# The first twenty weight loads of a fused attention and feed-forward kernel, each issued as two transfers of 64 partitions

## The chip, the cores and the metric

The kernel runs on one core of a Trainium2 chip. The metric is the device time of one execution in microseconds, and lower is better. Three runs of the kernel before gave 1049.2, 1049.21 and 1049.95 us, with a median of 1049.21.

The core's engines go through their own instruction streams in order and meet at semaphores: TensorE (PE) multiplies, and loads its stationary operand beside that (PEld); VectorE (DVE) and ScalarE (ACT) work element by element; SyncE (SP) issues nearly all the DMA transfers. Sixteen DMA engines move the data between HBM and the 128 partitions of the on-chip memory.

## The reference

The first part is a linear attention over 8 batches, 8 heads and 576 positions of 64 numbers, with 256 features for each position:

```python
def phi(x):
    proj = np.einsum('bhsd,df->bhsf', x, w_phi)
    proj = proj - np.max(np.abs(proj), axis=-1, keepdims=True)
    return np.concatenate([np.exp(proj), np.exp(-proj)], axis=-1)
q_p, k_p = (phi(q), phi(k))
kv = np.einsum('bhsf,bhsd->bhfd', k_p, v)
z = np.sum(k_p, axis=2)
num = np.einsum('bhsf,bhfd->bhsd', q_p, kv)
den = np.einsum('bhsf,bhf->bhs', q_p, z)[..., None] + 1e-06
attn_out = (num / den).astype(np.float32)
```

Its output, as 4608 tokens of 512 numbers, goes through a feed-forward layer whose two weight matrices (512 x 2048 and 2048 x 512) arrive in float64:

```python
h = x @ w_in
sp = np.where(h > 20.0, h, np.log1p(np.exp(np.minimum(h, 20.0))))
g = h * np.tanh(sp)
out = (g @ w_out).astype(np.float32)
```

## The kernel before

**The two stages.** Keys and queries are loaded in units of 512 positions (`load_raw`, tiles `raw_k` and `raw_q`, 256 KB). TensorE projects a unit (`pp_k`, `pp_q`), VectorE finds the largest magnitude (`m_k`, `m_q`) and subtracts it (`e_k`, `e_q`), and ScalarE takes the exponentials. Key features times values (`v`, 330 KB a batch and pair of heads) are summed on TensorE in `kvps` and copied to `kv`. Query features are turned (`dt`), multiplied with `kv` (`num`), and divided on VectorE (`r`, `x`). The result is turned to `xt` and split into a high part `xTh` (ScalarE) and a low part `xTl` (VectorE). The feed-forward stage works on 18 chunks of 256 tokens, each with 16 column tiles: `h` is x times w_in, `u` its activation, `o` the product with w_out. Each factor is held in a high and a low part, so that one product takes three. From the fourth chunk on, `o` is formed from sums and differences of blocks (`ox`, `oy`, `oz`, `ow`), for which sums of the weights are made on the chip, kept in HBM (`terms`) and loaded again.

**The weights.** They come as 32 pieces, 16 of w_in (`words_in`) and 16 of w_out (`words_out`), of 128 rows of 512 float64 numbers: 4 KB a partition, 512 KB a piece. `load_weight` (L242) brings the words of a piece. For 29 of the pieces `load_middle` (L246) brings a second copy, shifted by 16 bits, into one of three homes (`middle_in`, `middle_out`, 4092 bytes a partition), so that VectorE can take the lower bits of the mantissa from it. For each piece ScalarE takes the magnitude of the high words (L251, waits for the words). VectorE then clamps (L265), shifts the middle copy (L270, waits for it), shifts (L278), sets the sign (L283, waits for the words), cuts out the power of two (L288) and writes the low part of the weight (L293). ScalarE writes the high part (L312). A home is free for the next shifted copy when L293 of the piece before is done, and SP waits for that.

**What sets the order.** A planner (class `Plan`) simulates the engines with a table of due times and durations and then writes out the order of every engine's instructions, loads included. It plans one task for each load of words or of a shifted copy. `load_weight` and `load_middle` are called in the planned order, and what a task issues does not change the plan. SP goes through its list in order: an instruction that has to wait holds up all those behind it.

**The semaphores of the transfers.** The transfers of SP and ScalarE take eight semaphores in turn (DMAHW0 to DMAHW7). A transfer that would take a semaphore again first waits until the transfer that had it before has landed. So at most eight are under way, and the ninth is issued when the first has landed. Each transfer is spread over the sixteen DMA engines.

**The first 60 us.** SP issues keys, queries and values first, and the first words (`words_in`) at 5.91 us. Until 22 us it issues the words of the first nine pieces and the shifted copies of the first three among queries and values. The shifted copies of further pieces wait for a home from 29.84 us on. TensorE works on attention until the first `h` at 46.8 us.

Of the kernel before, what the change touches and what calls it, by code (L numbers as in the profile page):

```python
# [10 lines left out]
U32 = mybir.dt.uint32  # L11
U16 = mybir.dt.uint16
# [5 lines left out]
P = 128  # L18
# [41 lines left out]
NFIRST = 6  # L60
NTRIAL = 3
NLOADS = 11
VLATE = 4.5
E0 = 0.138
E1 = 0.171
# [20 lines left out]
class Plan:  # L86
# [11 lines left out]
    def order(self):  # L98
# [85 lines left out]
        tasks = [task for _, _, task in issued]  # L184
        at = [n for n, task in enumerate(tasks) if task["name"].startswith("load ")][:NLOADS]
        loads = sorted(range(NLOADS), key=lambda i: i + VLATE * tasks[at[i]]["name"].startswith("load v"))
        for n, task in zip(at, [tasks[at[i]] for i in loads]):
# [5 lines left out]
def attention_then_mish(ctx, tc, qT, kT, va, w_phi, w_in, w_out, out):  # L193
    nc = tc.nc
# [28 lines left out]
    def slot_tile(slot, dtype, name, words=None):  # L223
        return const.tile([P, words] if words else [P, 2, 512], dtype, tag=slot, name=name)
# [11 lines left out]
    def octets(kind, i, j):  # L236
        return w_in[i * P:(i + 1) * P, j * 512:(j + 1) * 512] if kind == "in" else w_out[i * P:(i + 1) * P, :]

    def load_weight(kind, i, j):
        nm = f"{kind}_{i}_{j}"  # L240
        words = weight[kind, i, j] = slot_tile(f"w{nm}", U32, f"words_{nm}").rearrange("p a b -> p (a b)")
        nc.sync.dma_start(words, octets(kind, i, j).bitcast(U32))  # L242

    def load_middle(kind, i, j, home):
        middle = middles[kind, i, j] = slot_tile(home, U16, f"middle_{kind}_{i}_{j}", 2048)
        nc.sync.dma_start(middle[:, :2046], octets(kind, i, j).bitcast(U16)[:, 1:2047])  # L246

    def magnitude(kind, i, j):
        w = to_add[kind, i, j] = scratch(f"w_{kind}_{i}_{j}", f"w:{(kind, i, j)}", U32)
# [687 lines left out]
    for i, pc in enumerate(pieces):  # L937
        nm, slot = f"{pc}", slots[i]
        ahead = [f"split {pieces[i - NAHEAD]}"] if i >= NAHEAD else []
        used = [f"split {pieces[n]}" for n in range(nmiddle) if homes[n % len(homes)] == slot]  # L940
        add(f"load {nm}", "SP", -47.5 + i * 0.1, 0.42, lambda pc=pc: load_weight(*pc),
            deps=last_use.get(slot, []) + used, after=ahead, take=[(slot, f"w:{nm}")], size=524288)
        if i < nmiddle:
            home = homes[i % len(homes)]
            add(f"middle {nm}", "SP", -47.45 + i * 0.1, 0.42, lambda pc=pc, home=home: load_middle(*pc, home),
                deps=last_use.get(home, []), take=[(home, f"m:{nm}")], size=524288)
        add(f"abs {nm}", "ACT", WKEYS[i] - 0.5, 0.55, lambda pc=pc: magnitude(*pc), deps=[f"load {nm}"], take=[("w", f"u:{nm}"), ("part", f"w:{nm}")])
        def split(step, took, fn, deps, **more):
            add(f"{step} {nm}", "DVE", WKEYS[i], took, lambda pc=pc, fn=fn: fn(pc), deps=deps, late=0.13, **more)

        own = i >= nmiddle
        split("clamp", 0.34, split_clamp, [f"abs {nm}"])
        split("rest", 0.95 if own else 0.34, split_rest, [f"load {nm}" if own else f"middle {nm}"],
              take=[("part", f"rest:{nm}"), ("half", f"t:{nm}")] if own else [])
        split("shift", 0.34, split_shift, [f"clamp {nm}"])
        split("sign", 0.61, split_sign, [f"shift {nm}"])
        split("power", 0.34, split_power, [f"sign {nm}", f"rest {nm}" if own else f"middle {nm}"])
        split("split", 0.61, split_low, [f"power {nm}", f"rest {nm}"], give=[f"rest:{nm}", f"t:{nm}"] if own else [f"m:{nm}"])
        add(f"ready {nm}", "ACT", WKEYS[i] + 0.1, 0.55, lambda pc=pc: high_weight(*pc), deps=[f"sign {nm}", f"power {nm}"], give=[f"u:{nm}", f"w:{nm}"])
# [188 lines left out]
```

## Time and profile before

| | |
|---|---|
| median of three runs | 1049.21 us |
| the profiled execution | 1048.77 us |
| its span (first to last instruction) | 1047.0 us |
| granted TensorE clock, mean | 0.998 |
| DMA engines busy | 64.4% of the span with the load and store queue (q1) |
| instruction queues | 97 packets, 1.59 MB (q8), and 40 packets, 0.33 MB (q14) |
| HBM read and written | 177.59 MB and 43.52 MB |

The page gives each engine's busy time in the span. Idle time of an engine matters only where it holds up the chain that ends last, so the chain of waits tells more than the shares. "issue" in it is time in which an engine waited for nothing that the profile shows. Rows of the timeline give start and duration of a group of instructions, the engine, the line of the kernel, the operation, what is written and read, and in brackets the engine's idle time before it and what ended it. "SPq" are transfers that SP issues, with the time the issue took. The DMA views give for a stretch each queue's packets, bytes and share of the sixteen engines, and for each kind of transfer issued in it the time from issue to landing. Views of a stretch sort the rows by start. By these views a load issued between 9 and 22 us landed 8 to 10 us later, and one issued between 30 and 60 us landed 3 to 8 us later.

### The profile page before, as it was taken

How to read it: one execution, taken by the hardware profiler on the slowest of the kernel's cores; microseconds unless marked ns; L12 is line 12 of the kernel's file. 1: busy time of each engine (PE TensorE's matmuls, PEld its weight loads, DVE VectorE, ACT ScalarE, POOL GpSimd, SP SyncE). 2: the span in 40 equal slices, each digit the busy share in tenths (PEclk: the TensorE clock that was granted, in tenths of full speed). 3: DMA queues.
4: the chain of work that ended last, by engine and by line, in shares of the span. 5: the costliest groups of instructions: out<-in, count | busy, mean ns of one | idle time of the engine just before them, and what ended most of it. 6: DMA issues, size and time to landing. Idle time of an engine off the chain costs nothing.

```text
span 1047.0 us, 30038 instructions
## 1 busy us (share of the span) xinstructions
PE 1029.5 (98%) x12286; PEld 989.7 (95%) x12286; DVE 739.3 (71%) x1695; ACT 658.1 (63%) x1027; POOL 0.7 (0%) x6
## 2 busy tenths in 40 slices
PE   8899999999999999999999999999999999999998
PEld 7788889989889999999999999999999999999998
DVE  7898989678886675767676767675776666666553
ACT  7699897666665756666666656665666565545532
POOL 0000000000000000000000000000000000000000
PEclk9999999999999999999999999999999999999999
DMA  9768654455976666767667564757576656765844
GB/s 338 241 228 318 198 178 158 135 180 161 300 253 231 216 203 205 235 205 236 213 203 235 184 215 154 245 187 242 174 225 212 205 187 212 223 225 179 290 142 152
DMA packets 156297, 223.09 MB, mean 213 GB/s; under 512 B 16896, under 2 KB 74112, under 8 KB 156160
## 3 DMA queue, kind: packets, MB, share of 16 engines
q1 hardware_dynamic: 156016, 221.11, 64.4%
q8 instruction: 97, 1.59, 0.6%
q14 instruction: 40, 0.33, 0.1%
q10 hardware_dynamic: 144, 0.07, 0.0%
HBM read 177.59 MB, written 43.52 MB: 211 GB/s over the span
## 4 chain that ended last, share of the span: by engine, by line
PE 92%; DVE 3%; ACT 2%; DMA 2%; issue 1%; SPq 0%; DVEq 0%; ACTq 0%
PE h L561 38%; PE o L596 8%; PE oy L729 8%; PE ox L729 8%; PE ow L729 8%; PE kvps L387 7%; PE num L387 6%; PE oz L729 4%; PE pp_q L346 4%; PE pp_k L346 3%; DMA terms<-comb 1%; DMA raw_k<-kT 0%; DMA raw_q<-qT 0%; PE dt L466 0%; ACT e_k L372 0%
## 5 line engine op out<-in xcount | busy, mean ns | idle before, releaser
L561 PE MATMUL h<-xTh,win 128*128 128x256 f32 x2304 | 430.4, 281 | 1.0 <-DVE e_k L358 1.0
L561 PEld LDWEIGHTS h<-xTh,win 128*128 128x128 f32 x2304 | 362.1, 188 | 5.3 <-PE h L561 1.2
L561 PE MATMUL h<-xTl,win 128*128 128x256 f32 x1152 | 322.3, 280 | 0.0
L561 PEld LDWEIGHTS h<-xTl,win 128*128 128x128 f32 x1152 | 217.1, 188 | 1.8
L646 DVE TENSOR_TENSOR sl<-s,sh 128x640 fp32r<-128x640 f32 x112 | 92.0, 823 | 107.1 <-ACT sh L642 102.5
L642 ACT CAST sh<-s 128x640 fp32r<-128x640 f32 x112 | 80.8, 723 | 90.6 <-DVE s L637 79.0
L627 ACT ACTIVATE u<-h 128x512 f32<-128x512 f32 x112 | 67.0, 598 | 95.9 <-PE h L561 95.4
L635 DVE TENSOR_TENSOR s<-u 128x256 f32<-128x256 f32 x112 | 46.9, 419 | 90.6 <-ACT u L627 90.4
L387 PEld LDWEIGHTS kvps<-v,e_k 128*64 128x64 f32 x2560 | 78.2, 137 | 8.1 <-issue 4.3
L729 PE MATMUL oy<-wout,sh 128*128 128x256 f32 x448 | 85.8, 284 | 0.0
L387 PE MATMUL kvps<-v,e_k 128*64 128x66 f32 x2560 | 83.7, 223 | 1.9 <-issue 1.9
L729 PE MATMUL ox<-wout,gh 128*128 128x256 f32 x440 | 83.6, 282 | 0.0
L729 PE MATMUL ow<-wout,sh 128*128 128x256 f32 x440 | 82.9, 281 | 0.0
L596 PE MATMUL o<-wout,gh 128*128 128x512 f32 x256 | 81.8, 400 | 0.0
L387 PE MATMUL num<-kv,e_q 128*64 128x66 f32 x2304 | 76.8, 223 | 3.0 <-issue 1.3
L387 PEld LDWEIGHTS num<-kv,e_q 128*64 128x64 f32 x2304 | 71.7, 137 | 6.3 <-issue 2.9
L422 ACT ACT_TABLE_LOAD x25 | 32.1, 1283 | 64.9 <-DVE e_k L358 64.6
L729 PEld LDWEIGHTS oy<-wout,sh 128*128 128x128 f32 x448 | 68.4, 188 | 1.6
L729 PEld LDWEIGHTS ox<-wout,gh 128*128 128x128 f32 x440 | 67.3, 188 | 0.7
L729 PEld LDWEIGHTS ow<-wout,sh 128*128 128x128 f32 x440 | 67.4, 188 | 0.0
L729 PE MATMUL oy<-wout,sl 128*128 128x256 f32 x224 | 62.8, 281 | 0.0
L729 PE MATMUL ox<-wout,gl 128*128 128x256 f32 x220 | 61.7, 281 | 0.0
(119 smaller groups left out, 1826.2 us busy)
## 6 DMA issues: line engine op xcount, KB each, us to landing
wout<-terms SPq DMA_DIRECT2D x344, 256.0 KB, 4.6
there_e<-e_q SPq DMA_DIRECT2D x60, 256.0 KB, 2.7
e_q<-there_e SPq DMA_DIRECT2D x240, 64.0 KB, 2.2
v<-va SPq DMA_DIRECT2D x32, 330.0 KB, 4.4
raw_q<-qT SPq DMA_DIRECT2D x36, 256.0 KB, 3.5
out<-osb SPq DMA_DIRECT2D x35, 256.0 KB, 2.6
raw_k<-kT SPq DMA_DIRECT2D x34, 256.0 KB, 3.2
words_in<-w_in SPq DMA_DIRECT2D x16, 512.0 KB, 5.8
```

The source lines that it names most:

```text
L346: nc.tensor.matmul(ps[j][:, n], raw[rows, n * P:(n + 1) * P], w_phi2[rows], start=True, stop=True)
L387: nc.tensor.matmul(ps[rows], lhsT[h], rhs[h], start=start, stop=stop, skip_group_check=True)
L422: nc.scalar.activation(e[:, 1, :], e[:, 0, :], AF.Exp)
L561: nc.tensor.matmul(ps, w[:, wcol], x[:, cc % 2, :], start=(n == 0), stop=(n == 11))
L596: nc.tensor.matmul(ps.rearrange("p (k n) -> p k n", k=2), g[:, cols], w, start=(i == first and k == 0), stop=(i == end and k == 2))
L627: nc.scalar.activation(u, h_live.pop((c, fp)).rearrange("p f s -> p (f s)"), AF.Mish)
L635: nc.vector.tensor_tensor(s[:, :CH], u[:, :CH], u[:, CH:], op=ALU.add)
L642: nc.scalar.copy(mix_high[c, fp], mixed[c, fp])
L646: nc.vector.tensor_sub(mix_low[c, fp], mixed.pop((c, fp)), mix_high[c, fp].bitcast(F32))
L729: nc.tensor.matmul(banks_of[c][k][:, half], a, b, start=(begins and n == half == 0), stop=(ends and n == 2), skip_group_check=True)
```

## The change

`load_weight` and `load_middle` hand their transfer to a new helper, `in_parts`. For the first 20 calls it issues two transfers, of partitions 0 to 63 and 64 to 127; after that it issues one of 128 partitions as before. Bytes, rows and places in memory are the same.

```diff
+NHALVED = 20
...
+    nissued = [0]
+
+    def in_parts(to, src):
+        nissued[0] += 1
+        rows = P // 2 if nissued[0] <= NHALVED else P
+        for at in range(0, P, rows):
+            nc.sync.dma_start(to[at:at + rows], src[at:at + rows])
+
     def load_weight(kind, i, j):
         nm = f"{kind}_{i}_{j}"
         words = weight[kind, i, j] = slot_tile(f"w{nm}", U32, f"words_{nm}").rearrange("p a b -> p (a b)")
-        nc.sync.dma_start(words, octets(kind, i, j).bitcast(U32))
+        in_parts(words, octets(kind, i, j).bitcast(U32))
 
     def load_middle(kind, i, j, home):
         middle = middles[kind, i, j] = slot_tile(home, U16, f"middle_{kind}_{i}_{j}", 2048)
-        nc.sync.dma_start(middle[:, :2046], octets(kind, i, j).bitcast(U16)[:, 1:2047])
+        in_parts(middle[:, :2046], octets(kind, i, j).bitcast(U16)[:, 1:2047])
```

The calls are counted in the planned order: the twenty are twelve loads of words and eight of shifted copies, and before the change they were issued between 5.91 and 50.93 us. The order of the program shows two places. The first is SP from the first load of words on, where the full stretch of DMA begins. Tiles are named by kind and column block with a running number. Before:

```order
L242 DMA words_in_0_105<-w_in 128x1024 [waits DMAHW4_49]
L417 DMA v_107<-va 128x660 [waits DMAHW5_49]
L417 DMA v_109<-va 128x660 [waits DMAHW6_49]
L417 DMA v_121<-va 128x660 [waits DMAHW7_49]
L246 DMA middle_in_0_123<-w_in 128x2046 [waits DMAHW0_49]
L242 DMA words_in_0_125<-w_in 128x1024 [waits DMAHW1_49]
L338 DMA raw_q_1_135<-qT 128x512 [waits DMAHW2_49]
L246 DMA middle_in_0_147<-w_in 128x2046 [waits DMAHW3_49]
L242 DMA words_in_0_149<-w_in 128x1024 [waits DMAHW4_49]
```

The same place of the changed program:

```order
L246 DMA words_in_0_105<-w_in 64x1024 [waits DMAHW4_49]
L246 DMA words_in_0_105<-w_in 64x1024 [waits DMAHW5_49]
L426 DMA v_108<-va 128x660 [waits DMAHW6_49]
L426 DMA v_110<-va 128x660 [waits DMAHW7_49]
L426 DMA v_122<-va 128x660 [waits DMAHW0_49]
L246 DMA middle_in_0_124<-w_in 64x2046 [waits DMAHW1_49]
L246 DMA middle_in_0_124<-w_in 64x2046 [waits DMAHW2_49]
L246 DMA words_in_0_127<-w_in 64x1024 [waits DMAHW3_49]
L246 DMA words_in_0_127<-w_in 64x1024 [waits DMAHW4_49]
L347 DMA raw_q_1_138<-qT 128x512 [waits DMAHW5_49]
L246 DMA middle_in_0_150<-w_in 64x2046 [waits DMAHW6_49]
L246 DMA middle_in_0_150<-w_in 64x2046 [waits DMAHW7_49]
```

Nothing changes its place; each load of a piece takes two of the eight semaphores, one after the other, so that the transfers behind it wait for later landings. The second place is SP behind the first pause, where shifted copies wait for VectorE and queries stand behind them. Before:

```order
L246 DMA middle_in_0_580<-w_in 128x2046 [waits DMAHW5_49,DVE_49]
L246 DMA middle_out_0_596<-w_out 128x2046 [waits DMAHW6_49,DVE_49]
L338 DMA raw_q_0_599<-qT 128x512 [waits DMAHW7_49]
L338 DMA raw_k_604<-kT 128x512 [waits DMAHW0_49]
L417 DMA v_625<-va 128x660 [waits DMAHW1_49]
```

And changed:

```order
L246 DMA middle_in_0_592<-w_in 64x2046 [waits DMAHW1_49,DVE_49]
L246 DMA middle_in_0_592<-w_in 64x2046 [waits DMAHW2_49]
L246 DMA middle_out_0_609<-w_out 64x2046 [waits DMAHW3_49,DVE_49]
L246 DMA middle_out_0_609<-w_out 64x2046 [waits DMAHW4_49]
L347 DMA raw_q_0_613<-qT 128x512 [waits DMAHW5_49]
L347 DMA raw_k_618<-kT 128x512 [waits DMAHW6_49]
L426 DMA v_639<-va 128x660 [waits DMAHW7_49]
```

Two more issues now stand ahead of the queries. On TensorE, VectorE and ScalarE the instructions and their order are the same; those that read a halved load wait for two of the eight semaphores where they waited for one.

## The prediction

> **What bounds the kernel now.** The page comes first.
>
> ```profile
> span 1047.0 us, 30038 instructions
> PE 1029.5 (98%) x12286; PEld 989.7 (95%) x12286; DVE 739.3 (71%) x1695; ACT 658.1 (63%) x1027; POOL 0.7 (0%) x6
> ```
>
> TensorE is busy nearly all the time, so loads can move the end only where TensorE stands still. The twenty loads of the change are issued between 5.9 and 51 us, so the view I read next is the chain of waits between 20 and 47 us, before the first feed-forward products (start us, us, what). Of its longest pieces:
>
> ```profile
> 21.31 1.27 issue
> ...
> 27.32 1.66 issue
> 29.37 1.02 PE dt L466 x8
> ...
> 33.99 1.27 DVE m_q L350 x2
> ```
>
> The chain hangs on TensorE until 34 us and then passes to VectorE. Two of its pieces, 2.9 us together, are "issue": TensorE stands still and nothing that the profile records is late. Busy times between those stops (the stretches 16.11 to 22.59 and 22.59 to 28.97, whole core; PE and PEld with counts, then DVE, ACT, POOL, the clock, the DMA share and the rate) tell what they are:
>
> ```profile
> 16.11:22.59 6.48, 5.20 (x127) 4.71 (x127) 4.83 (x12) 6.13 (x19) 0.00 (x0) 1.00 1.03 415
> 22.59:28.97 6.38, 4.73 (x126) 4.39 (x127) 5.86 (x16) 4.18 (x10) 0.00 (x0) 1.00 1.01 399
> ```
>
> From one stop to the next TensorE ran 254 and 253 recorded instructions (waits aren't counted): a fixed block of about 256. DMA was full meanwhile, 1.01 to 1.03 of sixteen engines. The DMA views of short stretches show the block coming. Rows of six stretches in turn: 16.11 to 20.20, 20.20 to 20.40, 22.59 to 26.50, 26.50 to 26.70, then 28.97 to 30.20 and 30.20 to 30.40 us (queue and kind, packets, MB, share of sixteen engines):
>
> ```profile
> q1 hardware_dynamic: 538, 1.71, 103.6%
> ...
> q8 instruction: 1, 0.02, 33.8%
> ...
> q1 hardware_dynamic: 511, 1.59, 103.4%
> ...
> q8 instruction: 1, 0.02, 34.2%
> ...
> q1 hardware_dynamic: 58, 0.20, 39.5%
> ...
> q8 instruction: 1, 0.02, 39.5%
> ```
>
> After TensorE enters a block at 16.11, no instruction packet moves until 20.20; after 22.59, none until 26.50. TensorE runs out at 21.31 and 27.32 and resumes at 22.59 and 28.97, some 2.3 us after the packet starts. After 28.97, with the load queue 39.5% busy, the packet comes within 1.4 us. So the fetch of the next block waits 3.9 to 4.2 us behind loads, and 1.4 us or less without them. The difference, about 2.7 us, is what the loads cost the fetch.
>
> **What the change does, part by part.** Order of the program: TensorE, VectorE and ScalarE run the same instructions as before. SP issues 20 more transfers, and eight semaphores are still handed out in turn, so eight transfers can be under way, of 256 KB where they were of 512.
>
> *The bytes.* They are the same, in the same order. In the full stretch the queue is far deeper than eight halves need:
>
> ```profile
> words_in<-w_in SPq DMA_DIRECT2D x1, 512.0 KB, 9.3
> 14.00:20.00 6.00, 5.79 (x152) 5.30 (x150) 5.33 (x14) 5.62 (x13) 0.00 (x0) 1.00 1.02 402
> ```
>
> The load of words issued at 12.51 took 9.3 us to land; at 402 GB/s a 512 KB load moves in 1.30 us and a half in 0.65. Eight halves are 5.2 us of work, against about 2 us from issue to landing of a lone 64 KB transfer (2.0 in the row below on e_q). The queue stays full, and a load lands when it did: 0.
>
> *The fetch's turn.* The ring holds 9 us of loads, yet the fetch waits 4: it doesn't stand behind everything, but takes turns with the load ring. 2.7 us is 2.1 times 1.30, the time in which each engine moves its share of one 512 KB load. I read the wait as two turns of one whole load's share each. With halves a turn is 0.65 us and the wait falls by 1.35. Bounds from both sides: 0, if the fetch waits behind a fixed number of bytes whatever transfer they belong to; 2.7, if it would find no load ahead at all. I take 1.35, because the wait is so near a whole number of shares.
>
> [...]
>
> *What the shorter wait is worth.* The stop at 21.31 was 1.27 us: with the block 1.35 earlier it goes. TensorE enters the next block 1.27 earlier, asks that much earlier, and waits 1.35 less for it: of the 1.66 us stop 0.3 is left. Sum 1.27 + 1.35 = 2.6 us. Does the rest keep up?
>
> ```profile
> 19.25 4.24 ACT L372 ACTIVATE e_k<-pp_k,mm_k 128x128 f32<-128x128 f32 x16
> 22.97 0.16 DVE L509 TENSOR_SCALAR r<-num 128x4 f32<-128x4 f32 x1 [1.36 <-PE num L387]
> 31.59 0.69 DVE L545 TENSOR_TENSOR xTl<-xt,xTh 128x512 fp32r<-128x512 f32 x1 [1.17 <-ACT xTh L539]
> 33.97 1.29 DVE L350 TENSOR_REDUCE m_q<-pp_q 128x4 f32<-128x512 f32 x2 [0.69 <-PE pp_q L346]
> ```
>
> VectorE stands idle for TensorE's results at 22.97 and 33.97 and, through ScalarE, at 31.59, 3.2 us in all: it can follow. ScalarE ends the exponentials at 23.49, just before the products of kvps would begin (24.93 less 1.27 is 23.66). So the 2.6 reaches 34 us, and the VectorE work behind it is moved as a whole. Bounds: 1.3, if one of the two turns is shortened (0.65 off each stop), and 2.9, if both stops go.
>
> *SP's time.* Rows on SP (start us, us); the landing of the queries issued at 31.93 and their use on TensorE; and the tightest of the later halved loads, issued at 50.93 and used at 56.72:
>
> ```profile
> 4.49 0.43 SPq L338 DMA_DIRECT2D raw_k<-kT  x1
> 4.97 0.43 SPq L417 DMA_DIRECT2D v<-va  x1
> 29.84 0.33 SPq L246 DMA_DIRECT2D middle_in<-w_in  x1
> 30.45 1.43 SPq L246 DMA_DIRECT2D middle_out<-w_out  x1
> 31.93 0.43 SPq L338 DMA_DIRECT2D raw_q<-qT  x1
> raw_q<-qT SPq DMA_DIRECT2D x1, 256.0 KB, 5.6
> 41.06 1.23 PE L346 MATMUL pp_q<-w_phi,raw_q 64*128 64x128 f32 x16
> 50.93 0.33 SPq L246 DMA_DIRECT2D middle_in<-w_in  x1
> middle_in<-w_in SPq DMA_DIRECT2D x1, 511.5 KB, 3.7
> 56.72 0.42 DVE L270 TENSOR_SCALAR middle_in<-middle_in 128x512 uint32<-128x512 uint32 x1
> ```
>
> Back to back, one issue costs SP 0.48 us. Up to 22 us SP waits for its semaphores between issues (a load lands 9 us after its issue, and eight are under way), which hides the added ones. Behind the two loads of shifted copies at 29.84 and 30.45 the queries (31.93) would be issued 0.96 later; they land at 37.5 and are used at 41.06, 3.5 later, so the cost is 0. (With TensorE 2.6 earlier the cover is 0.9, but the two loads wait for VectorE, which is then also 1.3 or more earlier.) At 50.93 the second half goes out 0.48 later; the load landed at 54.6, 2.1 ahead of its use: 0. Without cover each would cost its 0.5 us. I allow 0 to 0.5, and take 0.2.
>
> Sum: 1048.77 (the profiled execution) - 2.6 + 0.2 = 1046.4. The median of the runs is 0.44 above that execution, so 1046.8.
>
> **Rivals.**
>
> *The fetch waits behind a fixed depth of bytes.* Then both stops stay, and all else is hidden: 1049.2, with 0 to 0.5 for SP. For it speaks that a half's packets are of the same 4 KB rows, and that 2.1 shares may as well be some 17 rows. Against it, only the near whole number.
>
> *A half doesn't run at full rate.* If sixteen engines that write only 64 partitions get in each other's way and halves run at half rate, each halved load takes 2.6 us for 1.3. Fourteen of them lie ahead of the queries issued at 31.93: 18.2 us more, of which the slack of 3.5 takes up a part, and the 2.9 us of stops of today another. TensorE would stand still for some 12 us more, and the time is 1061. It decides from the point where a halved load costs over 0.25 us more (3.5 over 14), about 340 GB/s. What speaks against it is the fetch of four pieces of 64 KB into 32 partitions each, which stood behind other loads and ran out in one go from 939.20 to 940.00, and a lone such piece (issued at 172.95):
>
> ```profile
> q1 hardware_dynamic: 508, 0.26, 112.4%
> 939.20:940.00 0.80, 0.80 (x9) 0.80 (x9) 0.64 (x3) 0.47 (x1) 0.00 (x0) 1.00 1.12 327
> e_q<-there_e SPq DMA_DIRECT2D x1, 64.0 KB, 1.9
> ```
>
> Into a quarter of the partitions at a time, in rows of 512 bytes, the data went at 327 GB/s, far over half of 402. So I give the rival little.
>
> [...]
>
> *SP comes late.* The added 0.48 us an issue reach a consumer at one or two places after 30 us: 1049.7 to 1051, if the first forecast fails too.
>
> **How the numbers follow.** Shorter turns: 0.52, with 1046.8 and its own range 1045.9 to 1048.1. Fixed depth: 0.30, 1048.6 to 1049.9. Halves slow: 0.12, 1052 to 1061. SP late: 0.06. Range for 8 in 10: 1045.8 to 1050.6, which leaves out the slow halves and little else. What a measurement of this kernel can tell from no change is about 0.2%, 2.1 us. The first case passes it (gain over 2.1) about seven times in ten, so faster is 0.37; the rest of that case, the fixed depth and half of the late SP are the same, 0.48; slower is 0.15.
>
> **What would show it.** If right, "issue" in the first 30 us falls from some 3 us to under 1, the instruction packet starts within 3 us of the block's entry, the first m_q after 33 us starts near 31.4, and the rate from 14 to 20 us stays at 400 GB/s. If the stops are still 1.3 and 1.7 us, the turn isn't a transfer's share. A rate near 200 GB/s in that stretch and words landing after 40 us would mean that the halves are slow. TensorE waiting for raw_q at its third or fourth use would put the blame on SP. Above all the forecast is wrong if the packet starts earlier and the stop stays, because something else feeds TensorE late.

## The result, and the profile after

The change makes the kernel slower: a median of 1060.91 us (six runs, 1059.03 to 1062.59) against 1049.2 us before. The ratio is 1.011, with a 95% interval of 1.0095 to 1.0125. The profiled execution took 1062.59 us. It is 13.8 us behind that of before, and its n-th product on TensorE shows where: number 500 starts 7.4 us later than before, number 800 (at 52 us before) 11.3, number 1500 (at 108 us) 13.9, and the last ones 13.5. All is lost in the first 108 us, in the stretch that the prediction looked at, but with the other sign.

From the page of the kernel after: span, busy times, the DMA share and the rate in 40 slices of 26.5 us, and the chain by engine.

```profile
span 1060.8 us, 30081 instructions
PE 1036.1 (98%) x12286; PEld 995.3 (94%) x12286; DVE 739.8 (70%) x1695; ACT 656.9 (62%) x1027; POOL 0.7 (0%) x6
...
DMA  9988664445786757576757565757567655765844
GB/s 229 233 235 276 235 208 142 147 155 187 262 272 210 257 189 239 193 240 200 218 180 237 168 228 167 252 189 238 186 213 216 219 180 196 229 222 188 285 144 148
...
PE 85%; DMA 7%; ACT 3%; DVE 3%; SPq 1%; issue 1%; DVEq 0%; ACTq 0%
```

In the first two slices the DMA engines are busy at least nine tenths of the time and move only 229 and 233 GB/s. Busy and slow is the thing to see. Stretches of the kernel after (us, then busy times, clock, DMA share, GB/s):

```profile
14.00:20.00 6.00, 3.46 (x86) 3.09 (x88) 2.92 (x8) 4.03 (x8) 0.00 (x0) 0.99 1.04 246
20.00:22.00 2.00, 2.00 (x20) 1.78 (x22) 0.51 (x2) 1.01 (x2) 0.00 (x0) 0.50 1.05 230
38.00:40.00 2.00, 2.00 (x37) 2.00 (x38) 1.29 (x4) 1.91 (x4) 0.00 (x0) 0.50 1.03 240
56.00:60.00 4.00, 3.81 (x18) 3.85 (x19) 2.17 (x5) 2.42 (x5) 0.00 (x0) 0.50 1.06 227
```

The first row answers to the 402 GB/s of before; the others, with a granted clock of 0.50, are taken up below. The chain of waits of the kernel after (start us, us, what) no longer hangs on TensorE there:

```profile
4.96 6.42 DMA v<-va
...
11.40 9.99 DMA middle_in<-w_in
...
21.41 8.89 DMA middle_in<-w_in
...
30.32 9.24 DMA words_out<-w_out
...
39.57 9.28 DMA middle_in<-w_in
...
50.51 9.98 DMA middle_out<-w_out
```

Landing releases issue, through the eight semaphores, from 5 to 60 us (but for 1.4 us on VectorE at 48.9): the load stream sets the pace. TensorE's timeline of the kernel after, with idle time and what ended it in brackets, and SP's row for the queries, shows what that costs:

```profile
18.62 0.68 PE L396 MATMUL kvps<-v,e_k 128*64 128x66 f32 x14 [2.54 <-issue]
19.81 2.08 PE L355 MATMUL pp_k<-w_phi,raw_k 64*128 64x128 f32 x16
27.12 0.34 PE L396 MATMUL num<-kv,e_q 128*64 128x66 f32 x4 [1.73 <-issue]
35.70 0.39 PE L396 MATMUL kvps<-v,e_k 128*64 128x66 f32 x6 [3.85 <-issue]
42.83 0.48 SPq L347 DMA_DIRECT2D raw_q<-qT  x1
44.42 1.27 PE L396 MATMUL num<-kv,e_q 128*64 128x66 f32 x35 [1.15 <-issue]
52.96 1.17 PE L355 MATMUL pp_q<-w_phi,raw_q 64*128 64x128 f32 x16 [2.79 <-DMA raw_q<-qT]
```

The queries are issued at 42.83 and waited for until 52.96. Before, the same products ran at 41.06 without a wait: 11.9 us. The stops at the blocks did not go. They are four (the rows that wait for "issue") and sum to 9.3 us, where there were 2.9.

Standing still is only half of the loss. For the same 12286 products TensorE's busy time is 1036.1 us on this page and 1029.5 on the page of before, and the rest of the span 24.7 and 17.5 us: of the 13.8 us, 7.2 are waiting and 6.6 are products that took longer. Most of that is the granted clock: it is 0.50 in the last three stretches above, behind the three longest stops (which ended at 18.6, 35.7 and 53.0 us), and up to 72 us the rows of 4 us add up to 6.8 us of full speed withheld, against 1.7 before (an estimate). The 16 products of pp_k at 19.81 took 2.08 us; before, the same ones took 1.16 at 17.31. The kernel before has one such dip, a clock of 0.71 from 44 to 48 us. That the stops bring the clock down is inferred from this order, and no run varied it alone; the shorter stops (1.73 and 1.15 us) are not followed by a dip.

### The profile page after: what moved, and what is told of

Its sections match the earlier page's. It is cut to its first block, busy times and chain, and to the rows that moved or that the text cites. A ratio compares the mean times of both kernels' runs of the same rounds, so it can differ in the third digit from the quotient of the medians.

```text
span 1060.8 us, 30081 instructions
## 1 busy us (share of the span) xinstructions
PE 1036.1 (98%) x12286; PEld 995.3 (94%) x12286; DVE 739.8 (70%) x1695; ACT 656.9 (62%) x1027; POOL 0.7 (0%) x6
## 3 DMA queue, kind: packets, MB, share of 16 engines
q8 instruction: 97, 1.59, 0.6%
## 4 chain that ended last, share of the span: by engine, by line
PE 85%; DMA 7%; ACT 3%; DVE 3%; SPq 1%; issue 1%; DVEq 0%; ACTq 0%
PE h L570 36%; PE oy L738 8%; PE ox L738 8%; PE ow L738 7%; PE o L605 6%; PE num L396 5%; PE kvps L396 5%; PE oz L738 4%; DMA middle_in<-w_in 3%; PE pp_q L355 3%; PE pp_k L355 2%; DMA middle_out<-w_out 1%; DMA words_out<-w_out 1%; DMA v<-va 1%; ACT L576 1%
```

## The experiments

Two theories at first. **Halves:** a load that writes only one half of the partitions, 0 to 63 or 64 to 127, is slow. **Small transfers:** the loss is due to 256 KB transfers, their number, or SP's issues. The kernel before, timed on the same chip each time, took 1049.44 us beside the first kernels below (up to the first twelve loads), 1049.54 beside those with even and odd partitions and with four column parts, and 1050.31 beside the two with quarters. Each ratio is against its own; it comes from all runs and is not the quotient of the two medians.

### Streams of loads alone

Sixteen loads back to back, one shape after another:

```python
nc.sync.dma_start(t[:, :1024], piece(i))                             # whole piece
nc.sync.dma_start(t[:, :512], piece(i // 2)[:, col:col + 512])       # column halves
nc.sync.dma_start(t[at:at + 64, :1024], piece(i // 2)[at:at + 64])   # halves, at = 0, 64 in turn
nc.sync.dma_start(t[:64, :1024], piece(i // 2)[at:at + 64])          # always the low half
nc.sync.dma_start(t[odd::2, :1024], piece(i // 2)[odd::2])           # even, odd partitions
```

Further streams are the 64 rows of a half spread over 128 partitions; 32 partitions by 8 KB, quarter by quarter; halves of w_in; halves from two issuing engines; and 64 KB blocks.

> Left out: the whole computation (the output is zeros). The kernel is streams of sixteen loads each, one behind the other, with only the shape of a load different, and the rate of each stream is read once it is full. Theories of the slow halves. [...] Smaller transfers (S): whatever is 256 KB, column halves and respread ones too, near 235; whole pieces near 400. Read side (R): the 64 rows read together are slow: halves and respread ones 235, column halves near 400. [...]

Steady stretches of that kernel: the five shapes of the code, then the 64 rows spread out, the quarters, and the halves of w_in (VectorE, GpSimd, clock, DMA share, GB/s):

```profile
16.00:23.00 7.00, 0.00 (x0) 0.00 (x0) 1.00 1.01 404
36.00:40.00 4.00, 0.00 (x0) 0.00 (x0) 1.00 1.03 386
50.00:61.00 11.00, 0.00 (x0) 0.00 (x0) 1.00 1.03 231
72.00:86.00 14.00, 0.00 (x0) 0.00 (x0) 1.00 1.04 210
99.00:103.00 4.00, 0.00 (x0) 0.00 (x0) 1.00 1.02 380
115.00:119.00 4.00, 0.00 (x0) 0.00 (x0) 1.00 0.97 369
127.00:136.00 9.00, 0.00 (x0) 0.00 (x0) 1.00 1.02 219
160.00:173.00 13.00, 0.00 (x0) 0.00 (x0) 1.00 1.01 226
```

Column halves (386), every second partition (380) and a half's rows spread over 128 partitions (369) run at nearly the full 404 GB/s, with the same 256 KB a transfer. Small transfers and the read side are out: what is slow is writing to one half at a time (231 in turn, 210 always low). Two parts told nothing. ScalarE ran ahead, so that its high halves moved beside the quarters and not beside the low halves; and the streams of six 64 KB blocks were too short to be steady. Both are taken up again below.

### The same twenty loads, split by columns

```diff
-        rows = P // 2 if nissued[0] <= NHALVED else P
-        for at in range(0, P, rows):
-            nc.sync.dma_start(to[at:at + rows], src[at:at + rows])
+        cols = (512 if to.shape[1] == 1024 else 1024) if nissued[0] <= NHALVED else to.shape[1]
+        for at in range(0, to.shape[1], cols):
+            end = min(at + cols, to.shape[1])
+            nc.sync.dma_start(to[:, at:end], src[:, at:end])
```

> The same twenty loads in two transfers each, as many transfers and bytes under way as in the change, but split by columns: 128 partitions by 2 KB. [...] Smaller transfers, their number or SP's issues (S): the rate stays near 235 and the time near 1060.

1050.28 us, ratio 0.9995 (0.9978 to 1.0012): the loss is gone, with as many transfers as in the change. The stretch of 14 to 20 us:

```profile
14.00:20.00 6.00, 4.94 (x117) 4.44 (x118) 4.41 (x12) 4.60 (x9) 0.00 (x0) 1.00 1.04 386
```

### Which of the twenty cost

```diff
-        rows = P // 2 if nissued[0] <= NHALVED else P
+        rows = P // 2 if 12 < nissued[0] <= NHALVED else P
```

for the later eight, and for the first twelve

```diff
-        rows = P // 2 if nissued[0] <= NHALVED else P
+        rows = P // 2 if nissued[0] <= 12 else P
```

> Partition halves only for the 13th to the 20th of the twenty loads (issued from about 28 us on). [...] If the loss comes only from the start of the program (the first products waiting for words): 1049.

> Partition halves only for the first twelve loads. [...] If the loss came from the later eight: 1049 to 1051.

The later eight: 1048.77 us, ratio 0.9997 (0.9987 to 1.0007), near the 1049 of a loss that comes only from the start of the program. The first twelve: 1055.75 us, ratio 1.0053 (1.0038 to 1.0068), above the 1049 to 1051 of a loss from the later eight. All twenty cost 11.7, so the parts don't add: the later eight are free only as long as the loads ahead of them are on time. Their stretch, 32 to 40 us, was filled to 0.76 before (275 GB/s); now it is

```profile
32.00:40.00 8.00, 7.00 (x154) 5.97 (x152) 7.18 (x20) 5.72 (x13) 0.00 (x0) 1.00 0.96 257
```

so idle DMA time took up the slower rate. In the kernel with the first twelve halved the chain stays on TensorE, and its pieces called issue are

```profile
16.20 1.54 issue
...
22.93 3.19 issue
...
32.39 2.05 issue
...
40.43 2.13 issue
```

8.9 us against 2.9. The difference looks like the whole loss of that run, 6 us, but by the pages it is not. The span of its profile is 6.7 us longer, of which TensorE's busy time has 4.0 (1033.5 for 1029.5) and its waiting 2.7, since other waits shrank; the granted clock is 0.72 from 26 to 32 us and 0.79 from 40 to 48. With twelve the late instruction fetch is on the chain, and with twenty late data is. What each of them costs, and what the lower clock, was not separated.

### Which partitions make a load slow

A second kernel of streams, and the change itself with even and odd partitions in place of low and high. In the streams:

```python
nc.sync.dma_start(t[32:96, :1024], piece(i // 2)[at:at + 64])        # partitions 32 to 95
nc.sync.dma_start(t[:32, :1024], piece(i // 4)[at:at + 32])          # partitions 0 to 31
```

Further streams put two loads of 8 partitions by 8 KB ahead of halves in turn, or of the low half alone, and run the 64 KB blocks as the kernel fetches them, alone and behind three whole pieces. In the whole kernel:

```diff
-        rows = P // 2 if nissued[0] <= NHALVED else P
-        for at in range(0, P, rows):
-            nc.sync.dma_start(to[at:at + rows], src[at:at + rows])
+        step = 2 if nissued[0] <= NHALVED else 1
+        for at in range(step):
+            nc.sync.dma_start(to[at::step], src[at::step])
```

> Left out: the whole computation (the output is zeros). Streams of sixteen loads again. [...]

> The same twenty loads in two transfers of 64 partitions each, but the even partitions in one and the odd ones in the other. [...] If any transfer of 64 partitions is slow in this program: 235 GB/s and 1060.

Steady stretches of the streams: halves in turn, 32 to 95, 0 to 31, halves behind the two small loads, the low half behind them; then the first and the second microsecond of four 64 KB blocks behind whole pieces:

```profile
32.00:45.00 13.00, 0.00 (x0) 0.00 (x0) 1.00 1.04 232
57.00:61.00 4.00, 0.00 (x0) 0.00 (x0) 1.00 1.03 418
68.00:74.00 6.00, 0.00 (x0) 0.00 (x0) 1.00 1.01 204
84.00:95.00 11.00, 0.00 (x0) 0.00 (x0) 1.00 1.04 232
106.00:117.00 11.00, 0.00 (x0) 0.00 (x0) 1.00 1.04 207
148.80:149.80 1.00, 0.00 (x0) 0.00 (x0) 1.00 1.03 333
149.80:150.80 1.00, 0.00 (x0) 0.00 (x0) 1.00 0.66 132
```

Sixty-four neighbouring partitions run at 418 GB/s if they straddle the middle, and 32 partitions (204) do as well as 64 of one half (210). So neither the number of partitions nor neighbouring rows matter, but on which side of partition 64 they lie. Steady streams from one issuing engine whose loads each stay on one side ran at 204 to 232 GB/s, and those whose loads each reach both sides at 369 to 418 (404 for whole pieces, 418 for 32 to 95, 380 for every second partition). Why that is so, no run shows. Two small loads ahead of the halves, meant to have some engines write one half while the others write the other, gained nothing (232); whether they set any engines apart stays open.

Even and odd partitions in the whole kernel: 1049.42 us, ratio 0.9998 (0.9984 to 1.0013), and full rate in the same stretch:

```profile
14.00:20.00 6.00, 6.00 (x146) 5.48 (x148) 5.96 (x14) 5.35 (x12) 0.00 (x0) 1.00 1.04 414
```

Two transfers of 64 partitions each cost nothing where each reaches both sides of partition 64.

### Two issuing engines, and the 64 KB blocks

Streams of 32 loads that SyncE and ScalarE issue in turn and begin together:

```python
(nc.scalar if i % 2 else nc.sync).dma_start(t[at:at + 64, :1024], piece(i // 2)[at:at + 64])
(nc.scalar if i % 2 else nc.sync).dma_start(t[:64, :1024], piece(i // 2)[at:at + 64])
block(t, i, 0, nc.scalar if i % 2 else nc.sync)
block(t, i, i // 2 % 4, nc.scalar if i % 2 else nc.sync)
```

> Left out: the whole computation (the output is zeros). Streams of 32 loads, issued by SyncE and ScalarE in turn and now begun together (in the first streams ScalarE ran ahead, so that its high halves ran beside the quarters and the low halves ran alone). [...] Whole pieces from one engine: 404 to 410.

Low from one and high from the other; low from both; blocks into partitions 0 to 31; blocks round the quarters; whole pieces:

```profile
4.00:35.00 31.00, 0.00 (x0) 0.00 (x0) 1.00 1.03 246
50.00:83.00 33.00, 0.00 (x0) 0.00 (x0) 1.00 1.04 209
97.00:104.00 7.00, 0.00 (x0) 0.00 (x0) 1.00 0.78 197
119.00:127.00 8.00, 0.00 (x0) 0.00 (x0) 1.00 0.69 195
144.00:168.00 24.00, 0.00 (x0) 0.00 (x0) 1.00 1.02 411
```

Both halves in two queues at once gain 18% over one half (246 against 209), more than in turn from one queue (231 and 232, 10% over 210) but far from the 411 of whole pieces: that both halves are queued does not bring the rate of loads that reach both sides. The blocks ran below 0.8 of the engines, so their rates show no limit, and where the 327 GB/s in the prediction came from stays open.

### What the instruction fetch waits behind

The twenty loads in four column parts each, and then, after the run with the first twelve halved, halves that are cut once more by columns (quarters, below), for the first twelve loads (the second piece of the diff) and for all twenty:

```diff
-        cols = (512 if to.shape[1] == 1024 else 1024) if nissued[0] <= NHALVED else to.shape[1]
+        cols = (256 if to.shape[1] == 1024 else 512) if nissued[0] <= NHALVED else to.shape[1]
...
+        rows = P // 2 if nissued[0] <= 12 else P
+        cols = (512 if to.shape[1] == 1024 else 1024) if nissued[0] <= 12 else to.shape[1]
```

> The twenty loads in four transfers each, split by columns: 128 partitions by 1 KB, 128 KB a transfer, so that eight transfers under way are 1 MB. If the instruction fetch waits behind what is under way or behind a number of rows, its wait falls from 4 us to 2.5 or less and both stops go: 1046.5, if the loads keep 350 GB/s. If it waits behind a fixed 1.1 MB whatever the rows are: stops stay, 1049 to 1050. SP needs 0.33 to 0.48 us an issue and a transfer moves in 0.32 at 402 GB/s, so SP may set the rate: 270 to 350 GB/s, words and queries up to 5 us late, 1050 to 1055.

> Open after the run with the first twelve loads in halves (1055.7): does TensorE lose its 6 us there because words and queries land late (D), or because the instruction fetch waits longer behind loads that drain at half rate (F)? There the stops at the blocks of 256 were 1.54, 3.19, 2.05 and 2.13 us against 2.9 in all before. Here the same twelve loads go in four transfers each, half of the partitions by half of the columns: the rate stays near 232 GB/s, but eight transfers under way are 1 MB and not 2. D: the words are as late as there, 1055 to 1056. F: the fetch waits behind 0.5 to 0.8 MB instead of 1.1, 3.4 to 4.7 us for 5.6, and the stops shrink by 4 to 8 us in all: 1048 to 1052.

> All twenty loads in four transfers each, half of the partitions by half of the columns. The chain of the change ran through landing after landing up to 60 us, so I expect late data here: D: 1058 to 1062, with short stops at the blocks but TensorE, VectorE and ScalarE waiting for words and queries. F alone (the fetch is the whole loss in the change too): 1049 to 1053.

Measured: 1056.75 us for four column parts (ratio 1.0061, 1.0041 to 1.0081), 1063.7 for twelve loads in quarters (1.0132, 1.011 to 1.0154), 1066.05 for all twenty (1.0145, 1.0125 to 1.0166), each above all that was expected of it. The rows on the first two kernels: the stretch of 14 to 20 us with four column parts; TensorE with twelve loads in quarters; and one kind of issue of the latter between 20 and 34 us (KB each, us to landing).

```profile
14.00:20.00 6.00, 6.00 (x168) 5.64 (x168) 5.48 (x14) 4.31 (x8) 0.00 (x0) 1.00 0.83 261
```

```profile
18.05 0.68 PE L399 MATMUL kvps<-v,e_k 128*64 128x66 f32 x14 [2.03 <-issue]
39.09 2.15 PE L358 MATMUL pp_q<-w_phi,raw_q 64*128 64x128 f32 x16 [5.90 <-DMA raw_q<-qT]
54.38 2.09 PE L358 MATMUL pp_q<-w_phi,raw_q 64*128 64x128 f32 x16 [6.03 <-DMA raw_q<-qT]
...
words_in<-w_in SPq DMA_DIRECT2D x8, 128.0 KB, 3.8
```

With the twelve in quarters one stop of 2.03 us is left where there were four, as the fetch theory said, but the time got worse, and the queue is no longer full (the DMA share from 20 to 26 us is 0.70). SP sets the pace there, as the chain of waits of that kernel shows:

```profile
21.43 0.59 SPq L249
...
34.11 0.59 SPq L249
```

In between one issue follows the other, with 0.04 us from one to the next and no landing on the chain: 128 KB in 0.63 us are at most 208 GB/s. With four column parts the chain is the same from 16.8 to 34.9 us, mostly with 0.43 us an issue, at most 279 GB/s: the case that its expectation had named, at a higher price than it said. The stops were traded for queries that TensorE waits twelve microseconds for. So the run shows that a shorter queue frees the fetch (after the entry at 24.52 the packet came within 1.3 us). It can't show what part of the 6 us the late fetch alone was, since the added issues also slowed the loads.

A depth can be estimated from the queue rows of stretches from a block's entry to the fetch: 35.75 to 41.6 and 41.6 to 41.8 us in the kernel after; 22.19 to 27.1 with column halves (2 KB rows); and 24.52 to 25.6 with twelve loads in quarters.

```profile
q1 hardware_dynamic: 422, 1.37, 103.7%
...
q8 instruction: 1, 0.02, 41.2%
```

```profile
q1 hardware_dynamic: 862, 1.57, 96.8%
```

```profile
q1 hardware_dynamic: 185, 0.30, 96.1%
```

The prediction's row for 22.59 to 26.5 before was 511 packets and 1.59 MB. If the first 1.3 us, the wait without loads, is taken off at the mean rate of each stretch, 1.06 MB remain before, 1.07 after and 1.15 with column halves; with little queued, about nothing remains. These rows look like a fixed depth of bytes near 1.1 MB (an estimate), whatever transfer they belong to.

But such a depth is not shown. Before and after have the same 4 KB rows, so some 16 rows an engine would do as well. And at other blocks less remains, with the DMA engines as busy: 0.5 MB before (1.02 MB moved from 11.27 to 13.85 us), 0.9 and 0.6 with even and odd partitions (1.40 from 16.46 to 19.85, 1.07 from 22.38 to 25.30), 0.6 with column halves (1.09 from 29.54 to 32.45). The filling of the queue can be estimated as bytes issued less bytes moved. It was 2.6 to 2.9 MB at the entries of 16.11 and 22.59 before, 1.3 to 1.6 in the kernel after, and 0.7 to 1.1 at the three of even and odd partitions and column halves just named, which fits their shorter waits; but it was 2.4 at that of 11.27 before, where little remained.

So what the fetch waits behind stays open. Shown is how long it waits: 4.5 to 5.9 us in the kernel after while the loads move at some 235 GB/s, 2.6 to 4.9 us behind loads at 320 to 419 GB/s (2.6 before at 11.27, 4.9 with column halves at 22.19), and 1.4 us or less with little queued.

## Why the prediction was wrong, point by point

**What bounds the kernel** was read rightly: TensorE, with stops at blocks of about 256 instructions (254 and 253 recorded between the stops of before) when the fetch is behind loads. Slower loads can therefore cost twice, by late data and by late instructions; products that run longer, mostly at a lower clock behind the stops, are a third cost (6.6 us here), which the prediction did not have.

**"The bytes": the step that failed.** The prediction put "a load lands when it did: 0". At some 235 GB/s a 512 KB load takes 2.23 us for 1.30, 0.93 more, because each of its two transfers writes one half only (231 GB/s in the stream of halves in turn, 404 in that of whole pieces). The queries landed 15.4 us later and were used 11.9 later. The ground for dismissing the rival was one stretch of 0.8 us at 327 GB/s into quarters of the partitions. It held four blocks of 64 KB that went round all four quarters, between other loads. In the second streams such blocks also start at 333 GB/s, in a microsecond whose bytes are mostly the last rows of whole pieces, while a steady stream into partitions 0 to 31 runs at 204. That blocks of different quarters ran side by side in that stretch is argued, not shown; the streams of blocks never filled the engines. A short mixed stretch is no measure of a steady rate.

**"The fetch's turn"** failed too. With halves of 0.65 us a share the wait should have been 2.65 us; it was 5.7 to 5.9 at four blocks. The near whole number of shares came from two waits; a third in the same profile, from 11.27 to 13.9 us with the load queue full, was 2.6 us, one share over the lone fetch. The rival of a fixed depth of bytes does better in the kernel after: the 1.06 MB of before at 235 GB/s are 4.5 us, with the 1.3 of a lone fetch 5.8. It does not do for all kernels: with even and odd partitions, halves at full rate, the waits of the same two blocks were 3.4 and 2.9 us instead of 4.2 and 4.0, shorter by 0.7 and 1.1 of the forecast 1.35, where a fixed depth would have left the first of them (the queue held an estimated 1.1 and 0.9 MB there). Neither rule, turns or a fixed depth, is shown.

**What the shorter wait is worth.** Even and odd partitions are the fair test of the forecast, halves at full rate. TensorE's stops sum to 1.3 us instead of 2.9 (0.72 and 0.56), and its products run 1.3 us ahead at 35 us and 1.9 at 108 us in the profiled execution. By the end they are 0.1 behind: single stops from 298 to 800 us, which lie elsewhere in each profile, took it back. The time is that of before. So even there 2.6 us did not arrive.

**SP's time** was sized rightly. With twenty more transfers by columns the ratio holds 1; the added issues are hidden. With four parts a load they are not, and SP sets the rate.

**The rival "a half doesn't run at full rate"** came true with its 1061, by errors that cancel. Its price of 1.3 us a load was too high (0.93, as halves in turn do 10% better than one half alone, 231 against 210). And it took 2.9 us of stops off, where the stops grew by 6.3; they did not add to the sum, since by the chain the landings set the pace and TensorE waited for the queries after them. It had TensorE standing still for some 12 us more, where that was 7.2, and 6.6 went to products that took longer. So it was right that the halves are slow, and the near hit of the time is luck. Its own signs, a rate near 200 (246 in the stretch named) and words landing after 40 us, are what the profile shows: the words of the ninth piece landed at 46.7 us instead of 31.4.

## What to carry to other kernels

Split a load so that each part still reaches both sides of partition 64: by columns (386 GB/s) or by even and odd partitions (380), but not into partitions 0 to 63 and 64 to 127 (231); a tile of 64 partitions that has a choice goes to 32 to 95 (418). Don't split so finely that the issuing engine sets the rate: 128 KB at 0.47 us an issue are 279 GB/s. Look for DMA shares near 1 at half the rate: here (1.04 at 246 GB/s, for 1.02 at 402 before) that was the sign of loads that write one half of the partitions. Look at what is queued ahead of an instruction fetch: loads at half rate delayed the code (5.9 us for 4.0 to 4.2) as well as the data. And compare TensorE's busy time before and after, not its stops alone: at a lower granted clock the same products take longer (2.08 us for 1.16 at 0.50).

## What the runs showed of the hardware that I had not expected

- Two halves in turn in one queue, or from two issuing engines, gain little: 231 and 246 GB/s against 404 to 411 for whole pieces. That is 10% over a single half (210) in one queue and 18% (209) in two.
- Partitions 32 to 95, 64 in a row, run at 418 GB/s.
- The fetch of TensorE's next block came 2.6 to 4.9 us after the entry into a block behind loads at 320 to 419 GB/s, and up to 5.9 us behind loads at 234 GB/s. What sets the wait stays open.
- Behind the three longest stops TensorE's granted clock read 0.50, and 16 products took 2.08 us for 1.16.
- Loads in parts of 128 KB into 128 partitions ran at 261 GB/s: by the chain SP's issues, 0.43 us and 0.04 between, follow each other without a wait.
